# Attention into routed experts into SwiGLU: attention's loads on two queues, and the first expert slot started within attention's last steps

## The chip, the cores and the metric

One core of a Trainium2 chip runs the whole kernel as one program. The metric is the device time of one execution in microseconds (us); lower is better. The engines are named as in the profile: PE (TensorE matmul), PEld (its weight load), DVE (VectorE), ACT (ScalarE), POOL (GpSimd, which also issues DMAs), SP (SyncE, which here only issues DMAs and reads registers).

## The reference

Three layers follow one another. Shapes: 4 batches, 8 heads, 576 positions, head size 64, so 2304 tokens of width 512.

```python
# 1. attention: heads 0-3 see the last 32 positions, heads 4-7 every 32nd position
scores = q @ k.T / 8, masked (local or strided), softmax over keys
x = attn @ v                                  # -> [2304, 512]
# 2. one expert of 8 for each token
e_idx = argmax(x @ w_gate + modality_bias[modality_id])
gate_w = softmax(...)[e_idx]
out[mask_e] = gate_w * (relu(x[mask_e] @ w1[e]) @ w2[e])     # w1 512x1024, w2 1024x512
# 3. SwiGLU on the RMS-normalised rows
xn = x / rms(x) * rms_g
out = (silu(xn @ w_gate2) * (xn @ w_val)) @ w_out            # 512 -> 1536 -> 512
```

## The kernel before

**Attention** runs over 32 steps. There are 8 units, a batch with its local heads (even units) or its strided heads (odd units); a unit has two head pairs, a pair two halves, and each (unit, pair, half) is a step. The loop at the end of `attention` has j from 0 to 34: with i = j - 2 it issues `p_transpose(i)`, `scores(j)`, `qk_transpose(j+2)`, a call of `task(j, 0)`, `av(i)`, `x_transpose(i-1)`, `softmax(j)` and `task(j, 1)`. Every engine works its instructions in the order in which the program issues them, so this loop is the order of the engines. "Step n" below is the stretch that begins with the mask matmul (L148) of `scores(n)`.

**Loads.** `load_qk(n)` and `load_v(n)` load q and k, or v, of pair n (0 to 15). All of them are issued by SP, in one queue. A q or k load is one DMA of 144 KB per head. A local v takes two DMAs per head, a strided v five per head (L96: four of 31.5 KB, one of 18 KB), ten for a pair. `load_v` is called with three pairs ahead (three `vt` buffers), pairs 0, 1 and 2 ahead of the first step. Four small loads for the router (`setup`: `g_sb`, `wg_sb`, `idi`, `b01`) are issued in step 0. POOL issues the stores of attention's output, `xd<-xr` (L212, L216).

**Side work.** When a batch is complete (`on_batch`), a generator starts that routes its tokens (`route`) and, from the second batch on, fills the table of an expert slot (`table_a`). `Side.step` advances the generators at each `task`; a number behind `yield` is the ticks to wait, two ticks a step. While attention runs their small operations go to POOL; in the steps behind the last scores (`over` set) they go to DVE. `table_a(0)` ends with `fetch_known`, which issues slot 0's first weight loads (`raw`, 1 MB each, two buffers, L838) on SP, then computes the slot's token list and gathers its x (`xg`, L843, POOL).

**Slot 0.** A slot is 512 tokens of one expert. `first_slot` splits weight chunks into high and low parts (`conv`, ACT `whi` L908 and DVE `wlo` L909), transposes the gathered x with PE (L899) and splits it (`x_part`: ACT `xhi`, DVE `xlo`). Then the slot loop computes 8 column chunks (`h_chunk`, L1000, 12 matmuls each) and 8 row chunks (`y_chunk`), with `conv` running six chunks ahead. In the steps behind the last scores, PE gets a dummy matmul (`busy`, L247) per step. Four more slots and a loop of variable length follow, then the SwiGLU stage.

## Time and profile before

| What | us |
|---|---|
| Median of 3 runs (847.76 to 850.15) | 848.25 |
| The profiled execution's own time | 851.77 |
| Its span | 850.1 |
| PE busy in the span | 820.1 (96%) |
| DVE, ACT, POOL busy | 498.9, 344.8, 168.6 |
| Step 0 to the first slot's first matmul | 7.83 to 150.26 |

The profile is one execution. Times within it count from the start of the span. A PE that is shown busy can still run at a lower clock: the granted clock stands beside it, 1.00 for 2.4 GHz and 0.50 for 1.2 GHz. A wait is read from who ended it, and the stretch in which it lies says what it is worth.

### The profile page before, as it was taken

What the parts mean: (1) busy time and instruction counts of PE and PEld (TensorE: products, weight loads), DVE (VectorE), ACT (ScalarE), POOL (GpSimd) and SP (SyncE); (2) the same over time, 40 slices, a digit from 0 to 9 for tenths busy, and PEclk for the clock granted to TensorE, in tenths of its full rate; (3) what the DMA queues carried; (4) which work ended last, traced back from release to release, by engine and by line L of the source; (5) the groups of instructions that cost most, each with busy time, mean ns of one, the idle gap of its engine ahead of it and who ended that gap; (6) DMA issues with size and microseconds to landing.
All of it is one profiled execution on the core that took longest, in us unless ns stands there. A gap on an engine that the chain in (4) does not pass through costs nothing.

```text
span 850.1 us, 12584 instructions
## 1 busy us (share of the span) xinstructions
PE 820.1 (96%) x4697; PEld 572.9 (67%) x4697; DVE 498.9 (59%) x1017; ACT 344.8 (41%) x748; POOL 168.6 (20%) x306
## 2 busy tenths in 40 slices
PE   9899997999997999999999999999999999999996
PEld 6788886787885888877566555655655565455565
DVE  4477767675434668575344465755756575564443
ACT  5477774435343564676252323231322323221111
POOL 4135565100202142021000100111111010112201
PEclk9699997999998999999999999999999999999999
DMA  8889575432518465263300101111111011001101
GB/s 141 150 167 176 126 176 152 149 100 101 199 49 283 137 228 198 100 211 87 101 26 1 50 2 48 50 51 49 51 50 36 15 53 47 1 1 74 62 26 62
DMA packets 94806, 80.48 MB, mean 95 GB/s; under 512 B 67990, under 2 KB 68502, under 8 KB 94742
## 3 DMA queue, kind: packets, MB, share of 16 engines
q1 hardware_dynamic: 87990, 64.89, 27.5%
q0 software_dynamic: 6752, 14.75, 5.6%
q8 instruction: 39, 0.64, 0.3%
q14 instruction: 25, 0.20, 0.1%
HBM read 64.84 MB, written 14.75 MB: 94 GB/s over the span
## 4 chain that ended last, share of the span: by engine, by line
PE 56%; issue 6%; DVE 2%; ACT 2%; DMA 2%; POOL 1%; SPq 0%; POOLq 0%; ACTq 0%
PE pg L1258 14%; PE ph L1258 13%; PE po L1292 5%; PE po L1290 5%; PE po L1291 5%; PE ph L1000 5%; PE py L1015 3%; PE py L1017 3%; PE py L1016 3%; DMA yd<-yb 1%; POOL out_dram L1301 1%; PE px L1115 1%; DVE u L1273 1%; ACT dt L435 1%; PE px L899 0%
## 5 line engine op out<-in xcount | busy, mean ns | idle before, releaser
L1277 ACT ACTIVATE ah<-u 128x512 fp32r<-128x512 f32 (+1 forms) x60 | 35.2, 587 | 273.2 <-DVE u L1273 273.2
L377 POOL TENSOR_TENSOR dt<-dt,ds 128x1024 int32<-128x1024 int32 x18 | 43.8, 2434 | 291.9 <-DVE dt L373 291.9
L1290 PE MATMUL po<-woh,ah 128*128 128x512 f32 x216 | 95.0, 440 | 0.2 <-ACT ah L1277 0.2
L1296 DVE TENSOR_TENSOR acc<-po,acc 128x512 f32<-128x512 f32 x72 | 49.6, 690 | 72.7 <-PE po L1292 72.7
L1292 PE MATMUL po<-woh,al 128*128 128x512 f32 x216 | 85.9, 398 | 0.0
L1291 PE MATMUL po<-wol,ah 128*128 128x512 f32 x216 | 85.2, 394 | 0.0
L1258 PEld LDWEIGHTS <-w1h 128*128 128x128 f16 x480 | 46.9, 99 | 46.3 <-ACT w1h L454 1.6
L1258 PEld LDWEIGHTS <-w0h 128*128 128x128 f16 x480 | 42.5, 99 | 49.4 <-issue 15.5
L1000 PE MATMUL ph<-xhi,whi 128*128 128x512 f32 x160 | 65.0, 406 | 6.2 <-SPq L869 5.7
L909 DVE TENSOR_TENSOR wlo<-raw,whi 128x512 fp32r<-128x512 f32 x80 | 60.8, 763 | 15.4 <-ACT whi L908 15.2
L1015 PE MATMUL py<-whi,hh 128*128 128x512 f32 x160 | 65.3, 408 | 0.0
L1000 PE MATMUL ph<-xlo,whi 128*128 128x512 f32 x160 | 63.9, 399 | 0.6 <-DVE xlo L902 0.6
L1000 PE MATMUL ph<-xhi,wlo 128*128 128x512 f32 x160 | 63.6, 398 | 0.0
L1017 PE MATMUL py<-whi,hl 128*128 128x512 f32 x160 | 62.9, 393 | 0.0
L1016 PE MATMUL py<-wlo,hh 128*128 128x512 f32 x160 | 62.6, 391 | 0.0
L1278 DVE TENSOR_TENSOR al<-u,ah 128x512 fp32r<-128x512 f32 (+1 forms) x60 | 38.3, 639 | 40.7 <-ACT ah L1277 40.7
L908 ACT ACTIVATE whi<-raw 128x512 fp32r<-128x512 f32 x80 | 49.5, 626 | 20.1 <-PE py L1017 16.3
L1007 DVE SCALAR_TENSOR_TENSOR hl<-ph,hh 128x512 fp32r<-128x512 f32 x40 | 27.6, 689 | 47.6 <-ACT hh L1006 47.4
L1290 PEld LDWEIGHTS po<-woh,ah 128*128 128x128 f32 x216 | 40.8, 189 | 12.9 <-ACT ah L1277 0.6
L169 ACT ACTIVATE P<-ps,nm 96x128 f32<-96x128 f32 (+1 forms) x176 | 48.4, 375 | 0.0
L1292 PEld LDWEIGHTS po<-woh,al 128*128 128x128 f32 x216 | 40.6, 188 | 10.8 <-DVE al L1278 1.5
L1006 ACT ACTIVATE hh<-ph 128x512 fp32r<-128x512 f32 x40 | 23.9, 598 | 56.6 <-PE ph L1000 54.9
(484 smaller groups left out, 1843.3 us busy)
## 6 DMA issues: line engine op xcount, KB each, us to landing
raw<-in_moe_w_dram SPq DMA_DIRECT2D x20, 1024.0 KB
w<-in_moe_w_gate_dram SPq DMA_DIRECT2D x6, 1024.0 KB
w<-in_moe_w_val_dram SPq DMA_DIRECT2D x6, 1024.0 KB
w<-in_moe_w_out_dram SPq DMA_DIRECT2D x6, 1024.0 KB
yd<-yb SPq DMA_DIRECT2D x5, 1030.0 KB
xg<-yd SPq DMA_DIRECT2D x18, 257.5 KB
qt<-in_q_dram SPq DMA_DIRECT2D x32, 144.0 KB
kt<-in_k_dram SPq DMA_DIRECT2D x32, 144.0 KB
```

The source lines that it names most:

```text
L169: nc.scalar.activation(P[0:nq, hh, t, 0:nk], pv[:, hh, t, :], AF.Exp, bias=nm[0:nq, hh, t:t + 1])
L908: nc.scalar.activation(hi, src, AF.Copy)
L909: eng.tensor_tensor(out=lo, in0=src, in1=hi.bitcast(F32), op=ALU.subtract)
L1000: nc.tensor.matmul(ps, a[:, kk, :], b_[:, kk, :], start=n == 0, stop=n == 3 * KD - 1)
L1015: nc.tensor.matmul(ys[t], hh[:, sl_], whi, start=m == 0, stop=False)
L1016: nc.tensor.matmul(ys[t], hh[:, sl_], wlo, start=False, stop=False)
L1017: nc.tensor.matmul(ys[t], hl[:, sl_], whi, start=False, stop=m == KF - 1)
L1258: nc.tensor.matmul(ps[:, 0:w], a[:, kk, 128 * mc:128 * mc + 128], b_[:, kk], start=i == 0, stop=i == 3 * KD - 1)
L1290: nc.tensor.matmul(ps, ah[:, sl_], woh, start=mc == 0, stop=False)
L1291: nc.tensor.matmul(ps, ah[:, sl_], wol, start=False, stop=False)
L1292: nc.tensor.matmul(ps, al[:, sl_], woh, start=False, stop=mc == MC - 1)
L1296: V.tensor_tensor(out=acc[:, t], in0=ps, in1=acc[:, t], op=ALU.add)
```

## The change

- Strided v loads are split: for the second head of a pair, in batches 0 to 2, POOL issues the five DMAs; SP keeps the rest.
- v is loaded four pairs ahead (four `vt` buffers). Pairs 2 and 3 are not loaded ahead of the first step but behind `load_qk(3)` and `load_qk(4)`, in steps 0 and 1. The four router loads move from step 0 to step 2, their first use from step 6 to step 7.
- The weight fetch of slot 0 becomes a generator of its own, `weights`, that waits until the last v load has been issued (`on_loaded`).
- Three `yield` counts in `route` and `table_a` are one tick shorter, and `first_slot` starts 6 ticks behind the gather instead of 8.
- `first_slot` now does the x transposes first. In the steps behind the last scores `task` runs `filler`: the first two column chunks (`FILL` = 2) of slot 0 in four pieces of six matmuls, between `p_transpose`, `av` and `x_transpose`, with attention's own PSUM banks. The slot loop takes these two chunks as done. The three dummy matmuls there are gone. `over` is set only when attention has ended, so `table_a(1)` runs on POOL.

```diff
@@ load_v
-            vt = v_t[u, hp] = ld.tile([128, 2, 6, D + 1], F32, name="vt", bufs=3)
+            vt = v_t[u, hp] = ld.tile([128, 2, 6, D + 1], F32, name="vt", bufs=4)
...
-                        nc.sync.dma_start(vt[0:18 * (R0[g + 1] - R0[g]), hh, g, 0:D],
-                                          v[b, h0 + hh].rearrange("(m r) d -> r m d", r=32)[R0[g]:R0[g + 1]])
+                        eng = nc.gpsimd if hh and b < B - 1 else nc.sync
+                        eng.dma_start(vt[0:18 * (R0[g + 1] - R0[g]), hh, g, 0:D],
+                                      v[b, h0 + hh].rearrange("(m r) d -> r m d", r=32)[R0[g]:R0[g + 1]])
@@ attention's loop
     load_v(1)
-    load_v(2)
...
                     load_qk(2 * steps[jj][0] + steps[jj][1] + 3)
-        task(j, 0, j >= NS)
+                    if jj in (1, 3):
+                        load_v(jj // 2 + 2)
+        if j < NS:
+            task(j, 0, False)
+        elif i < NS:
+            task(j, 0, True)
         if 0 <= i < NS:
             av(i)
             if steps[i][2] == 1:
-                load_v(2 * steps[i][0] + steps[i][1] + 3)
+                load_v(2 * steps[i][0] + steps[i][1] + 4)
+                if 2 * steps[i][0] + steps[i][1] + 5 == 2 * len(units):
+                    on_loaded()
+        if j >= NS and i < NS:
+            task(j, 1, True)
...
-        task(j, 1, j >= NS)
-        if j < 4 or j >= NS:
+        if j < NS:
+            task(j, 1, False)
+        if j < 4:
             busy(1)
@@ route: yield 4 -> 3; table_a: yield 3 -> 2, yield 4 -> 3
+        def weights(s):
+
+            while not loaded:
+                yield
+            known[0] = s + 1
+            fetch_known()
@@ table_a
-            known[0] = s + 1
-            fetch_known()
+            side.add(weights(s))
...
-                side.add(first_slot(), 8)
+                side.add(first_slot(), 6)
 
         def first_slot():
-            for i in range(AHEAD - 2):
-                conv(i)
-                yield 2
             xt[0] = x_new(xg.pop(0))
             for kk in range(KD):
                 x_part(xt[0], kk, bank)
-                yield 2
-            for i in range(AHEAD - 2, AHEAD):
+                if kk >= KD - FILL:
+                    conv(kk - KD + FILL)
+                yield
+            first_done.append(1)
+            for i in range(FILL, AHEAD):
                 conv(i)
                 yield
             first_done.append(1)
+
+        FILL = 2
+        NS_ = 4 * q.shape[0] * 2
+
+        def filler():
+            for m in range(FILL):
+                ps = bank()
+                xhi, xlo = xt[0][:2]
+                whi, wlo = conv_t.pop(m)
+                n = 0
+                for kk in range(KD):
+                    for a, b_ in ((whi, xhi), (whi, xlo), (wlo, xhi)):
+                        nc.tensor.matmul(ps, a[:, kk, :], b_[:, kk, :], start=n == 0, stop=n == 3 * KD - 1)
+                        n += 1
+                    if kk < KD - 1:
+                        yield
...
@@ task
-                if last and not over:
-                    over.append(1)
+                if last:
+                    if not fill:
+                        while not first_done:
+                            side.step(9)
+                        fill.append(filler())
+                    for _ in range((2, 2, 2, 2, 0)[2 * (j - NS_) + place]):
+                        next(fill[0], None)
+                    side.step(3)
+                    return
...
-                if j == 0:
+                if j == 2:
                     early.append(setup())
-                if j == 6:
+                if j == 7:
                     setup2(*early.pop())
@@ the slot loop
-                h.append(h_chunk(m, xt[s], conv_t.pop(i), tick))
+                if s == 0 and m < FILL:
+                    h.append(filled[m])
+                else:
+                    h.append(h_chunk(m, xt[s], conv_t.pop(i), tick))
```

The first place is SP's queue at the start, behind the loads of pairs 0 to 2 of q and k and of pairs 0 and 1 of v (`vt` is v, `qt` and `kt` are q and k; a number marks the buffer). Before, from the second head of v's pair 2 on:

```order
L96 DMA vt_240<-in_v_dram 126x1x64 x4
L96 DMA vt_240<-in_v_dram 72x1x64
L83 DMA qt_296<-in_q_dram 96x6x64 x2
L83 DMA kt_299<-in_k_dram 96x6x64 x2
L544 DMA g_sb_66<-in_moe2_rms_g_dram 128x4x1
L545 DMA wg_sb_114<-in_moe_w_gate_dram 128x4x8
L547 DMA idi_316<-in_moe_modality_id_dram 128x18x1
L549 DMA b01_318<-in_moe_modality_bias_dram 128x16
```

The same place of the changed kernel, directly behind v's pair 1:

```order
L83 DMA qt_284<-in_q_dram 96x6x64 x2
L83 DMA kt_287<-in_k_dram 96x6x64 x2
L97 DMA vt_290<-in_v_dram 126x1x64 x4
L97 DMA vt_290<-in_v_dram 72x1x64
L83 DMA qt_344<-in_q_dram 96x6x64 x2
L83 DMA kt_347<-in_k_dram 96x6x64 x2
L97 DMA vt_350<-in_v_dram 126x1x64 x4
L97 DMA vt_350<-in_v_dram 72x1x64
L554 DMA g_sb_66<-in_moe2_rms_g_dram 128x4x1
L555 DMA wg_sb_114<-in_moe_w_gate_dram 128x4x8
L557 DMA idi_407<-in_moe_modality_id_dram 128x18x1
L559 DMA b01_409<-in_moe_modality_bias_dram 128x16
```

q and k of pair 3 now stand ahead of all strided v, each strided pair has five DMAs here instead of ten, and the router loads stand behind q and k of pair 4.

The second place is PE behind the last scores (`P` and `PT` are the softmax output and its transpose, `xr` attention's output, `po` its PSUM bank). Before:

```order
L195 MATMUL po<-vt,PT 126x65 x2
L195 MATMUL po<-vt,PT 72x65 x2
L228 MATMUL pt<-ident,xr 128x126 x3
L181 MATMUL pt<-ident,P 126x126 x6
L195 MATMUL po<-vt,PT 126x65 x6
L228 MATMUL pt<-ident,xr 128x126
L228 MATMUL pt<-ident,xr 128x72
L247 LDWEIGHTS ones_b
L247 MATMUL pt<-ones_b 128x512
```

The same place of the changed kernel (`xg` is the gathered x of slot 0, numbered by token tile):

```order
L937 MATMUL pt<-ident,xg_2222 128x128
L196 MATMUL po<-vt,PT 126x65 x2
L196 MATMUL po<-vt,PT 72x65 x2
L229 MATMUL pt<-ident,xr 128x126 x3
L182 MATMUL pt<-ident,P 126x126 x6
L803 MATMUL pt<-xhi,whi 128x512
L803 MATMUL pt<-xlo,whi 128x512
L803 MATMUL pt<-xhi,wlo 128x512
```

The transposes of x, which stood behind all of attention, stand in steps 29 to 31, and chunk matmuls (L803, 24 in all, six at a time) between the last `p_transpose`, `av` and `x_transpose`.

The third place is DVE in steps 31 and 32. Before:

```order
L182 COPY PT<-pt 126x2x126 x2
L160 TENSOR_REDUCE nm<-ps 126x2x2
L203 TENSOR_SCALAR rs<-po 126x2
L204 RECIPROCAL rs<-rs 126x2
L205 TENSOR_TENSOR xr<-po,rs 126x128
L203 TENSOR_SCALAR rs<-po 72x2
L204 RECIPROCAL rs<-rs 72x2
L205 TENSOR_TENSOR xr<-po,rs 72x128
L182 COPY PT<-pt 126x3x126 x2
L909 TENSOR_TENSOR wlo<-raw,whi 128x512
```

The same place of the changed kernel, from `PT` of step 29 to shortly before that of step 30:

```order
L183 COPY PT<-pt 126x2x126 x2
L161 TENSOR_REDUCE nm<-ps 126x2x2
L681 RECIPROCAL wt<-sg 128x5
L684 TENSOR_SCALAR ao<-i128h,ra 128x128 x5
L940 TENSOR_TENSOR xlo<-pt,xhi 128x512
L947 TENSOR_TENSOR wlo<-raw,whi 128x512
L204 TENSOR_SCALAR rs<-po 126x2
L205 RECIPROCAL rs<-rs 126x2
L206 TENSOR_TENSOR xr<-po,rs 126x128
```

The splits of x and of the weights, and the last batch's `wt` and `ao`, now lie between attention's own operations.

## Rows read from the trace of the kernel before

**Rows 1.** PE's waits, 0 to 300 us: total, times, longest

```profile
PE ph L1000 <- SPq L869: 5.7, 1, 5.7
PE po L195 <- DMA vt<-in_v_dram: 3.8, 2, 2.3
PE pt L113 <- DMA kt<-in_k_dram: 2.1, 1, 2.1
PE pt L113 <- DMA qt<-in_q_dram: 1.9, 1, 1.9
```

**Rows 2.** Stretches: length, busy us (instructions) by engine, PEclk, DMA share, GB/s

```profile
20.69:43.89 23.20, 19.24 (x152) 17.07 (x151) 11.15 (x32) 11.21 (x34) 4.19 (x8) 0.71 0.86 149
20.69:30.53 9.84, 5.88 (x44) 5.18 (x43) 2.98 (x8) 3.52 (x11) 0.85 (x2) 0.65 0.98 154
30.53:36.67 6.14, 6.14 (x40) 5.59 (x39) 2.65 (x7) 3.50 (x11) 0.91 (x2) 0.50 0.79 133
59.19:73.67 14.48, 14.21 (x160) 12.66 (x159) 11.17 (x35) 11.35 (x38) 8.08 (x23) 1.00 0.61 131
47.60:77.38 29.78, 29.51 (x350) 25.82 (x349) 22.58 (x67) 22.95 (x75) 13.35 (x33) 1.00 0.74 153
128.27:157.63 29.36, 23.80 (x146) 18.44 (x144) 22.85 (x86) 13.44 (x33) 12.04 (x30) 0.83 0.45 137
139.20:147.28 8.08, 7.43 (x32) 5.48 (x33) 5.44 (x23) 2.33 (x5) 5.31 (x10) 0.53 0.21 44
201.62:204.42 2.80, 2.80 (x13) 2.26 (x12) 0.69 (x2) 1.35 (x3) 0.00 (x0) 1.00 0.00 0
```

**Rows 3.** SP's issues in order of time: start, length, line, operation, tiles

```profile
12.25 8.04 SPq L96 DMA_DIRECT2D vt<-in_v_dram  x10
20.42 0.93 SPq L83 DMA_DIRECT2D qt<-in_q_dram  x2
21.44 1.01 SPq L83 DMA_DIRECT2D kt<-in_k_dram  x2
...
124.46 1.02 SPq L838 DMA_DIRECT2D raw<-in_moe_w_dram  x2
125.59 13.55 SPq L96 DMA_DIRECT2D vt<-in_v_dram  x10
```

**Rows 4.** Two stretches of the start, columns as in rows 2

```profile
16.00:18.00 2.00, 2.00 (x26) 1.63 (x24) 1.54 (x5) 1.86 (x7) 0.33 (x1) 1.00 0.12 27
24.00:26.00 2.00, 0.64 (x3) 0.34 (x3) 0.00 (x0) 0.71 (x1) 0.00 (x0) 0.50 1.10 95
```

**Rows 5.** PE in order of time: slot 0's first and third column chunk

```profile
150.26 0.47 PE L1000 MATMUL ph<-xhi,whi 128*128 128x512 f32 x1
...
157.63 0.50 PE L1000 MATMUL ph<-xhi,whi 128*128 128x512 f32 x1 [0.52 <-DVE hl L1007]
```

**Rows 6.** DVE by line, 128.2 to 158.4 us: busy us, mean ns, idle before

```profile
L909 DVE TENSOR_TENSOR wlo<-raw,whi 128x512 fp32r<-128x512 f32 x8 | 5.5, 693 | 0.3 <-ACT whi L908 0.3
L182 DVE COPY PT<-pt 126x378 f32<-126x378 f32 (+1 forms) x8 | 3.6, 478 | 0.2 <-PE pt L181 0.2
L205 DVE TENSOR_TENSOR xr<-po,rs 126x384 f32<-126x384 f32 (+2 forms) x6 | 2.3, 379 | 0.2
L160 DVE TENSOR_REDUCE nm<-ps 126x6 f32<-126x756 f32 (+1 forms) x2 | 1.6, 809 | 0.1
L204 DVE RECIPROCAL rs<-rs 126x6 f32<-126x6 f32 (+2 forms) x6 | 1.0, 173 | 0.2
L203 DVE TENSOR_SCALAR rs<-po 126x6 f32<-126x6 f32 (+2 forms) x6 | 0.9, 157 | 4.3 <-PE po L195 4.2
```

**Rows 7.** POOL's DMA issues by line: ns min/median/max; the gather's time to landing

```profile
L212 POOL DMA_DIRECT2D xd<-xr x40: 605/622/709, 41.8 to 147.0; - x40
...
L843 POOL DMA_INDIRECT xg<-xd,idxA x8: 946/974/1201, 120.3 to 164.2; - x8
...
DMA to landing us min/median/max: 3.6/4.5/7.6
```

More of the change, by code (lines that the diff above doesn't have):

```diff
@@ L54, in make_consts, with attention @@
     return c
-def attention(ctx, tc, c, wk, q, k, v, xd, xcols, on_batch, task, set_banks):
+def attention(ctx, tc, c, wk, q, k, v, xd, xcols, on_batch, on_loaded, task, set_banks):
     nc = tc.nc
@@ L669, in route @@
             G.tensor_tensor(out=ra[:, t0:t1], in0=ra[:, t0:t1], in1=r1, op=ALU.add)
-            yield 4
+            yield 3
             V.reciprocal(wt[:, t0:t1, 0], sg)
@@ L724, in table_a @@
             G.tensor_tensor(out=base, in0=inc, in1=av, op=ALU.subtract)
-            yield 3
+            yield 2
             V.tensor_scalar(out=base, in0=base, scalar1=1.0, scalar2=None, op0=ALU.min)
@@ L738, in table_a @@
             G.tensor_tensor(out=early_n, in0=early_n, in1=new, op=ALU.add)
-            yield 4
+            yield 3
             blk = small("blka", NA)[:, 0:nt]
@@ L773, in first_slot @@
             first_done.append(1)
+        FILL = 2
[12 more added lines that the diff above has]
+                        yield
+                hh, hl = [xp.tile([128, XW], F32, name="xn", bufs=4)[:, 0:TS].bitcast(F32R) for p in "hl"]
+                nc.scalar.activation(hh, ps, AF.Relu)
+                V.scalar_tensor_tensor(out=hl, in0=ps, scalar=0.0, in1=hh.bitcast(F32), op0=ALU.max, op1=ALU.subtract)
+                filled.append((hh, hl))
+                yield
         def table_b(bank):
@@ L848 @@
         regs, raw_t, conv_t, xg, xt = {}, {}, {}, {}, {}
-        late, first_done, a_done = [], [], []
+        late, first_done, a_done, filled, fill, loaded = [], [], [], [], [], []
         known, waiting = [0], [0, 1]
@@ L966, in task @@
                     return
-                if j == 0:
+                if j == 2:
                     early.append(setup())
-                if j == 6:
+                if j == 7:
                     setup2(*early.pop())
                 side.step(3)
-            attention(pa, tc, c, wk, q, k, v, xd, xcols, on_batch, task, set_banks)
-            while not first_done:
+            attention(pa, tc, c, wk, q, k, v, xd, xcols, on_batch, lambda: loaded.append(1), task, set_banks)
+            over.append(1)
+            assert len(filled) == FILL
+            while len(first_done) < 2:
                 side.step(9)
```

## The prediction

> **What bounds the kernel now.** I read PE's waits first [rows 1], then the stretches around them [rows 2], then the queue that each wait names [rows 3, 4], and last the engines that share the end of attention [rows 5 to 7]. PE is the bound, with 820 of 850 us busy, and in the first 300 us it waits in three places only. At the start it waits 1.9 and 2.1 us for q and k of pair 3; near attention's end 3.8 us for v; and 5.7 us where the loop of variable length is entered, which the change doesn't touch [rows 1]. The reader is to see that the first two waits cost far more than their length. Steps 4 to 7 take 23.20 us; steps 12 to 15, the same work a batch later, take 14.48 [rows 2]. The difference is 8.7 us: 4.0 of it are the waits, the rest is the clock, which is 0.65 over the stretch with the wait and 0.50 over the 6.14 us behind it. At attention's end it is the same picture: behind the waits for v the clock is 0.53 for 8 us [rows 2].
>
> Both waits come from SP's queue. At 12.25 us SP begins ten DMAs of one strided v pair and needs 8.04 us to issue them, 0.80 each; q and k of pair 3 stand behind them and are issued at 20.42 and 21.44 [rows 3]. Meanwhile the DMA engines have little to do: from 16 to 18 us their share is 0.12 [rows 4]. So the shortage there is issue time, not bandwidth. At the end the order is the other way round: the last pair's v is issued behind 2 MB of weights and takes 13.55 us [rows 3].
>
> **The start.** q and k of pair 3 now directly follow v of pair 1, at about 12.25 us instead of 20.42: 8.2 us earlier, against waits of 4.0 us. With five DMAs instead of ten, v's pair 2 takes SP 4.0 us, so q and k of pair 4 stand at about 18.3. POOL issues the other half. The router's loads, in whose time the engines are full (share 1.10) at only 95 GB/s [rows 4], move behind q and k of pair 4 and no longer compete with pair 3. If both waits go, the clock has no reason to fall and the stretch returns to 14.48: 8.7 us. I take 8.0, since more loads now compete in the first 25 us. Bounds: 2 us, if half of the waits stays and the clock falls as before, and 9 us.
>
> **The second queue.** POOL gets 30 issues more, 5 for each of six pairs. The nearest row is its store of `xr`, of the same shape: 0.62 us, 0.71 at most [rows 7]. In a batch that is 6.2 us on top of 13.35 of 29.78 [rows 2], so POOL stays below two thirds; at the dearest row, the gather's 1.20 us, it would be 25.4, still below 29.78. These loads wait only for buffers that PE has just released, and are needed eight steps (29.8 us) later. I count nothing; POOL's own slack hides it. The Trainium skill speaks against it: "SBUF — State Buffer", section "SBUF: two separate sides", says that GpSimd can't write a DMA's descriptors while VectorE runs certain copies, and gives about 620 ns alone and 3100 ns beside one. The trace disagrees here: 40 issues lie between 605 and 709 ns while DVE is busy 22.58 of 29.78 us. By the page the 30 issues would be 93 us, an estimate, instead of 19; what that would do is the last rival.
>
> **The middle of attention.** Three `yield` counts are a tick shorter, so DVE asks POOL half a step (1.86 us) earlier for the ranks and tables, and what stands behind on DVE, the copy of `PT` for PE's next `av`, waits with it. DVE has 7.2 us idle in a batch. I take a loss of 0.5 us; bounds are nothing and 5.6 us (three times 1.86). A gain is excluded, since PE's work is the same.
>
> **Weights behind v.** The last two v pairs are issued in steps 23 and 25: 20 DMAs at 0.80 us, 16.1 us, or 4.3 steps of 3.72 us. The weights follow in step 27 to 28, earlier than before. Their first `wlo` stands in step 30, two to three steps later (some 9 us). All waits for v at the end go; next late would be these weights, or the gather. The gather is issued some 1.5 steps earlier than before, and the first x transposes ask for it three steps later, 11 us, where it takes 4.5 us to land, 7.6 at most [rows 7], behind 4 issues of about 1 us. Covered by some 2 us at worst.
>
> **The tail.** Measure from the scores of step 30 to the third column chunk: before, 128.27 to 157.63, 29.36 us [rows 2, 5]. In the changed kernel the same span holds the same PE work, now interleaved. Two floors:
> - PE: 23.80 us busy, of which 7.43 at a clock of 0.53; at full clock about 20.3.
> - DVE, by its new order: eleven 512-wide splits at 0.69 (7.6), eight `PT` copies at 0.478 (3.8), two maxima at 0.81 (1.6), six groups of sum, reciprocal and product at 0.709 (4.3), eight small ones at 0.16 (1.3): 18.6 us [rows 6].
>
> DVE can't run through: each filled chunk's split waits for its last six matmuls (1.4 us each, from 2.80 for twelve [rows 2]), and the last `x_transpose` waits for the last `xr`, about 1 us. That makes 22.4. PE also waits for DVE inside, at `av` of step 30, whose `PT` stands behind two weight splits and one x split: some 2 us, too short and too late to add to the DVE sum. One x transpose and the last batch's counting matmuls move ahead of my starting point, 1.0 us. The gain is 29.36 - 22.4 - 1.0 = 6.0 us. Bounds: 9.8, with DVE's bare 18.6, and nothing, if the waits bring the clock to half again.
>
> Behind that, the slot loop does two chunks less, so the generator that prepares the later slots has some six ticks less cover. It ends at the same place in the order as before, and its weights are converted six chunks (16.8 us) ahead of use. I count nothing; without that cover it would be two chunks, 5.6 us. The other edits (three dummy matmuls gone, `table_a(1)` on POOL) are in the sums.
>
> **Sum.** 8.0 - 0.5 + 6.0 = 13.5 us. The profiled execution would go from 851.77 to 838.3; the median shown is 3.5 us lower, and the same gain there gives 848.25 - 13.5 = 834.75, rounded 834.8.
>
> **Rivals.**
> - The tail gives nothing: DVE becomes the bound of steps 30 to 33, PE waits in pieces for `PT` and `xlo`, and the clock falls as it did at 139 us. For it: 18.6 us of DVE beside 20.3 of PE, both in one chain. Against it: no single wait should reach the 3.8 us of before. Only the start is left: 848.25 - 8.0 + 0.5 = 840.8.
> - The start stays bound by transfer: two queues bring no more bytes, and the late q and k are only replaced by late v. It gains 2, and the sum is 2 - 0.5 + 6.0 = 7.5: 840.8 too. Against it: the share of 0.12 [rows 4]. The Trainium skill, "DMA: Bandwidth & Descriptors", section "Issuing engines are not separate DMA queues", says that issuing from several engines saves only issue time, since all run on the same 16 DMA engines. By that rule a start short of bandwidth would give this time; the trace says issue time is what is short, so it decides nothing against the forecast.
> - The waits only move: v or x late in new places of the same weight. No change, about 848.
> - Slower: POOL's queue falls behind. POOL has 16.4 us idle in a batch; ten more issues fit while each takes less than 1.64 us. Above that POOL falls behind in each of two batches; ranks and stores come late, DVE stands waiting for POOL, and PE behind it. It turns the result at 2.3 us each, where two times 6.8 us make up the gain; at 2.6 us it is 9.6 us a batch, 19 in all, 834.8 + 19 = 854. Against it: 0.71 at most [rows 7].
>
> **How the numbers follow.** The forecast, with its own range of 830 to 839, gets 0.62. The tail without gain gets 0.16, the start without 0.10, waits that only move 0.05, POOL's queue 0.07. The first three are faster by more than 0.3% (2.5 us, about what a measurement of this kernel can tell from no change): 0.88. Within it: 0.05. Slower: 0.07. The range for 8 in 10 reaches from 829.5, the better bounds of both ends nearly together, to 842, which takes in the two rivals with half the gain.
>
> **What would show it.** Right: no wait for `qt` or `kt` near 22 us and a clock of 1.00 from 10 to 40 us; steps 4 to 7 near 14.5 us; no wait of `po` for `vt`; third column chunk some 13 us earlier than 157.6; POOL's v issues near 0.62 us. Wrong: a clock of 0.5 anywhere ahead of the third chunk, a wait of PE for DVE above 3 us in steps 30 to 33, `whi` or the x transposes waiting for DMA, or a longer wait behind the first slots that gives the gain back.

## The result, and the profile after

| | median | lowest to highest | profiled execution | its span |
|---|---|---|---|---|
| before | 848.02 us | 847.76 to 850.15 | 851.77 us | 850.1 us |
| after | 836.12 us | 835.58 to 838.78 | 838.78 us | 836.9 us |

With a fourth run the median before is 848.02 us, where the prediction had 848.25 of three.

The ratio is 0.986 (95% interval 0.9834 to 0.9887): 11.9 us faster, against 13.5 us forecast. The profiled execution lies 3.7 us above its median before and 2.7 after, so the traces differ by a little more, 13.2 us of span. The experiments further down ran on four chips on which the kernel before takes 857 to 859 us (below, the chip of this first measurement is called the first chip; at 848 us it is hardly one of the four). There the mean granted clock of one and the same kernel changes from execution to execution (before: 0.967 to 0.988), so single times spread by some 10 us, and only ratios to the kernel before, taken on the same chip, are compared (0.1% is 0.86 us).

**The waits.** PE's waits of the first 300 us in the kernel after (engine, tile and line, what it waited for; us in total, times, longest), to be held against [rows 1]:

```profile
PE ph L1047 <- SPq L907: 6.0, 1, 6.0
PE pt L937 <- DVE xlo L940: 1.8, 2, 1.3
PE pt L182 <- ACT xTb L236: 1.8, 2, 1.2
...
PE po L196 <- POOL ia L694: 1.1, 1, 1.1
PE pt L114 <- DVE PT L183: 0.7, 1, 0.7
...
PE pt L114 <- DMA qt<-in_q_dram: 0.2, 1, 0.2
```

The waits for `kt` and `vt` are gone, the one for `qt` is 0.2 us. The wait at the entry of the loop of variable length stays (6.0, before 5.7). New are the short ones for VectorE and ScalarE in attention's last steps, none above 1.3 us.

**The stretches.** The kernel after by stretches: from the scores of step 4 to those of step 8, on to step 26, to step 30, to the third column chunk, and the rest (columns: stretch, length, busy us and instructions of PE, PEld, DVE, ACT and POOL, PE's clock, DMA share, GB/s):

```profile
22.33:36.05 13.72, 13.72 (x153) 12.36 (x151) 10.19 (x28) 10.94 (x34) 4.15 (x8) 1.00 0.69 127
36.05:103.19 67.14, 66.34 (x779) 58.12 (x778) 52.31 (x165) 50.78 (x163) 46.07 (x112) 1.00 0.95 186
103.19:121.83 18.64, 17.87 (x217) 15.15 (x216) 12.06 (x37) 13.82 (x43) 7.74 (x11) 1.00 0.62 174
121.83:144.57 22.74, 17.72 (x130) 14.12 (x128) 16.50 (x47) 10.66 (x28) 16.84 (x49) 1.00 0.38 121
144.57:836.87 692.30, 675.59 (x3272) 452.93 (x3270) 395.29 (x705) 246.60 (x453) 101.40 (x129) 0.99 0.24 81
```

The first row answers to the 23.20 us and the fourth to the 29.36 us of [rows 2]. PE's clock is 1.00 in every stretch up to the third chunk, where before it was 0.65, 0.50 and 0.53 in places. PE has 5.0 us free in the fourth stretch, in pieces of at most 1.35 us, and the clock stays at 1.00 beside them.

**The queues.** SP's issues in the kernel after, at the start and at attention's end (start, duration, queue and line, tile, count), and below them all DMAs of the strided v by queue (min/median/max ns):

```profile
12.44 1.50 SPq L83 DMA_DIRECT2D qt<-in_q_dram  x2
14.04 1.73 SPq L83 DMA_DIRECT2D kt<-in_k_dram  x2
15.81 4.11 SPq L97 DMA_DIRECT2D vt<-in_v_dram  x5
20.04 1.83 SPq L83 DMA_DIRECT2D qt<-in_q_dram  x2
...
98.26 16.19 SPq L97 DMA_DIRECT2D vt<-in_v_dram  x20
116.90 31.69 SPq L876 DMA_DIRECT2D raw<-in_moe_w_dram  x4
```

```profile
L97 SPq DMA_DIRECT2D vt<-in_v_dram x50: 655/748/1003, 15.8 to 113.8; - x50
L97 POOL DMA_DIRECT2D vt<-in_v_dram x30: 597/626/852, 9.9 to 78.0; - x30
```

q and k of pair 3 go 8 us earlier than in [rows 3]. The last v pairs go ahead of the weights. An issue on POOL costs what its row of before let expect (0.62 us, [rows 7]).

**Where the time went**, worked out from the starts of the scores of each step in the two traces:

| stretch | before | after | gain |
|---|---|---|---|
| start to step 0 | 7.83 | 9.24 | -1.4 |
| step 0 to 4 | 12.86 | 13.09 | -0.2 |
| step 4 to 8 | 23.20 | 13.72 | 9.5 |
| step 8 to 26 | 66.54 | 67.14 | -0.6 |
| step 26 to 30 | 17.84 | 18.64 | -0.8 |
| step 30 to third chunk | 29.36 | 22.74 | 6.6 |
| third chunk to end | 692.43 | 692.30 | 0.1 |

The 1.4 us ahead of step 0 is not the change's: the last six dummy matmuls of the warm-up took 2.77 us in this execution and 1.53 before. In all experiments below step 0 begins between 7.4 and 7.8 us, also in those that start exactly as the changed kernel does.

### The profile page after: what moved, and what is told of

Same layout as the page of the kernel before. It is cut to its first block, busy times and chain, and to the rows that moved or that the text cites. A ratio compares the mean times of both kernels' runs of the same rounds, so it can differ in the third digit from the quotient of the medians.

```text
span 836.9 us, 12580 instructions
## 1 busy us (share of the span) xinstructions
PE 812.0 (97%) x4694; PEld 566.0 (68%) x4694; DVE 494.5 (59%) x997; ACT 344.4 (41%) x748; POOL 191.8 (23%) x356
## 4 chain that ended last, share of the span: by engine, by line
PE 59%; issue 6%; DVE 2%; POOL 1%; ACT 1%; DMA 1%; SPq 0%; POOLq 0%; ACTq 0%
PE pg L1308 14%; PE ph L1308 13%; PE ph L1047 7%; PE po L1342 5%; PE po L1340 5%; PE po L1341 5%; PE py L1062 3%; PE py L1064 3%; PE py L1063 3%; POOL out_dram L1351 1%; DMA yd<-yb 1%; PE px L1162 1%; DVE u L1323 1%; ACT dt L445 1%; PE px L937 0%
## 5 line engine op out<-in xcount | busy, mean ns | idle before, releaser
L1047 PE MATMUL ph<-xhi,whi 128*128 128x512 f32 x152 | 62.3, 410 | 6.0 <-SPq L907 6.0
L1062 PE MATMUL py<-whi,hh 128*128 128x512 f32 x152 | 62.0, 408 | 0.0
L1047 PE MATMUL ph<-xlo,whi 128*128 128x512 f32 x152 | 61.0, 401 | 0.0
L1047 PE MATMUL ph<-xhi,wlo 128*128 128x512 f32 x152 | 60.9, 401 | 0.0
L1064 PE MATMUL py<-whi,hl 128*128 128x512 f32 x152 | 59.7, 393 | 0.0
L1063 PE MATMUL py<-wlo,hh 128*128 128x512 f32 x152 | 59.5, 392 | 0.0
L1341 PEld LDWEIGHTS po<-wol,ah 128*128 128x128 f32 x216 | 40.7, 188 | 8.2
```

Of the source, the lines that this page charges most:

```text
L1047: nc.tensor.matmul(ps, a[:, kk, :], b_[:, kk, :], start=n == 0, stop=n == 3 * KD - 1)
L1062: nc.tensor.matmul(ys[t], hh[:, sl_], whi, start=m == 0, stop=False)
L1063: nc.tensor.matmul(ys[t], hh[:, sl_], wlo, start=False, stop=False)
L1064: nc.tensor.matmul(ys[t], hl[:, sl_], whi, start=False, stop=m == KF - 1)
L1341: nc.tensor.matmul(ps, ah[:, sl_], wol, start=False, stop=False)
```

## The experiments

Ratios are to the kernel before on the same chip, with their 95% intervals; times forecast in the expectations stand for a chip on which the kernel before takes 848 us. e1 to e4 ran on one chip, e5 to e8 on a second, e9 to e11 on a third, e12 on a fourth.

| run | ratio | interval | step 4 to 8 | step 8 to 26 | step 26 to third chunk, clock there |
|---|---|---|---|---|---|
| before (first chip) | 1 | | 23.20 | 66.54 | 47.20, 0.89 |
| after (first chip) | 0.986 | 0.983 to 0.989 | 13.72 | 67.14 | 41.38, 1.00 |
| e1 second queue alone | 0.992 | 0.989 to 0.996 | 13.82 | 69.47 | 48.62, 0.89 |
| e2 order alone, one queue | 0.999 | 0.996 to 1.003 | 13.96 | 81.83 | 50.29, 0.82 |
| e3 all of the loads | 0.990 | 0.983 to 0.996 | 13.73 | 67.33 | 45.30, 0.96 |
| e4 the end alone | 0.997 | 0.994 to 1.000 | 22.44 | 67.14 | 49.70, 0.83 |
| e5 the changed kernel again | 0.984 | 0.979 to 0.989 | 13.72 | 67.09 | 45.68, 0.93 |
| e6 without the two chunks | 0.989 | 0.984 to 0.993 | 13.72 | 67.23 | other work, see there |
| e7 all v on POOL | 0.994 | 0.990 to 0.998 | 14.07 | 72.13 | 43.45, 1.00 |
| e8 old yields | 0.985 | 0.978 to 0.991 | 13.72 | 66.68 | 46.56, 0.89 |
| e9 gather two and two, no gap | 0.982 | 0.978 to 0.985 | 13.81 | 67.23 | 44.87, 0.96 |
| e10 plain loads for the gather | 0.977 | 0.974 to 0.980 | 13.72 | 66.96 | 42.55, 0.92 |
| e11 router's loads early | 0.985 | 0.981 to 0.989 | 15.37 | 66.86 | 48.21, 0.86 |
| e12 gather two and two, with a gap | 0.975 | 0.973 to 0.978 | 13.72 | 67.06 | 43.60, 0.96 |

**e1: the second queue alone.** The kernel before with

```
-                        nc.sync.dma_start(vt[...], v[...])
+                        eng = nc.gpsimd if hh and b < B - 1 else nc.sync
+                        eng.dma_start(vt[...], v[...])
```

> The kernel before with one edit: five of the ten DMAs of each strided v pair (all but the last batch) are issued by POOL. Order of all loads, number of buffers and the end of attention as before. Theory (issue time on SP is what the first batch lacks): v of pair 2 takes SP 4.0 us in place of 8.04, so q and k of pair 3 are issued 4 us earlier, about 16.4 and 17.4 in place of 20.4 and 21.4; the two waits of 1.9 and 2.1 us shrink to a trace, the clock stays at 1.00, and most of the start's 8 to 9 us is gained by this edit alone: 839 to 841. Rival (order decides): the extra bytes in flight ahead of pair 3 and the router's loads behind it keep q and k late; at least one wait of over 1 us stays, and the gain is 0 to 3 us: 845 to 848.

SP's issues in e1 at the start, and its two stretches from step 4 to 8 and from step 8 to 26:

```profile
12.16 4.13 SPq L97 DMA_DIRECT2D vt<-in_v_dram  x5
16.42 0.93 SPq L83 DMA_DIRECT2D qt<-in_q_dram  x2
17.45 1.00 SPq L83 DMA_DIRECT2D kt<-in_k_dram  x2
```

```profile
20.44:34.26 13.82, 13.82 (x154) 12.45 (x152) 10.72 (x32) 10.98 (x34) 7.29 (x13) 1.00 1.05 165
34.26:103.73 69.47, 67.00 (x772) 57.87 (x770) 51.12 (x151) 50.66 (x163) 44.64 (x109) 1.00 0.86 173
```

The theory holds: with nothing but the issue time halved, q and k leave 4 us earlier, PE has no wait for them, and the start is as short as in the changed kernel, although the order and the router's loads are as before and the DMA share there is 1.05. What is lost behind, 2.9 us in the middle, sits in two steps (13 and 21) where ScalarE waits 1.85 and 1.83 us for POOL's `ex`; in e3, with the loads in the new order, it is gone. So the other edits of the loads (the order, the fourth buffer, the router's loads) have their worth too, but in the middle and not at the start; which of them it is was not run apart.

**e2: the new order with one queue.** The changed kernel with

```
-                        eng = nc.gpsimd if hh and b < B - 1 else nc.sync
+                        eng = nc.sync
```

> The changed kernel with the second queue taken away: all ten DMAs of every v pair on SP, in the new order, four pairs ahead. Theory (the order is worth most, the second queue little): q and k of pair 3 are issued at 12.4 us as in the changed kernel, so no wait for them; v of pair 2 now takes 8 us of SP, q and k of pair 4 stand at 24 in place of 20, v of pair 3 ends at 35 us and is first needed near 36: one short wait of 1 to 2 us there, 2 to 4 us over the changed kernel's time, 838 to 840. Rival (the second queue is what pays): the wait only moves to pair 4's q and k or pair 3's v, with the clock at half behind it as before, 6 to 9 us over the changed kernel, 842 to 845.

SP's issues in e2, and the stretches from step 4 to 8 and from step 8 to 9:

```profile
14.98 8.00 SPq L97 DMA_DIRECT2D vt<-in_v_dram  x10
23.09 0.94 SPq L83 DMA_DIRECT2D qt<-in_q_dram  x2
24.13 1.00 SPq L83 DMA_DIRECT2D kt<-in_k_dram  x2
25.17 7.81 SPq L97 DMA_DIRECT2D vt<-in_v_dram  x10
...
36.56 0.93 SPq L83 DMA_DIRECT2D qt<-in_q_dram  x2
```

```profile
20.49:34.45 13.96, 13.92 (x153) 12.40 (x152) 9.01 (x22) 10.97 (x34) 4.18 (x8) 1.00 0.50 117
34.45:46.34 11.89, 6.21 (x40) 5.46 (x39) 4.87 (x18) 2.70 (x10) 1.36 (x3) 0.69 1.08 159
```

The rival holds, and more than it says: of the gain nothing is left that can be measured. q and k of pair 3 are in time, but q and k of pair 5 stand behind twice 8 us of v and the router's loads; PE waits 4.8 us for them, the clock falls, and step 8 takes 11.89 us in place of 3.7 (before). The wait has moved by four steps with all that it costs. From step 24 to 30 the steps take about 7 us again; there PE waits 1.7 us for k and 2.2 us for ScalarE's `xTb`. The order alone only chooses which load is late; the second queue is what takes the lateness away.

**e3: all edits of the loads, nothing of the end.** The kernel before with e1's edit and

```
-vt = ... ld.tile([128, 2, 6, D + 1], F32, name="vt", bufs=3)
+vt = ... ld.tile([128, 2, 6, D + 1], F32, name="vt", bufs=4)
-    load_v(2)
+                    if jj in (1, 3):
+                        load_v(jj // 2 + 2)
-                load_v(2 * steps[i][0] + steps[i][1] + 3)
+                load_v(2 * steps[i][0] + steps[i][1] + 4)
-                if j == 0: ...setup()      if j == 6: setup2(...)
+                if j == 2: ...setup()      if j == 7: setup2(...)
```

> The kernel before with all edits of the loads (five of ten v DMAs on POOL, the new order at the start, four v buffers and four pairs ahead, the router's loads two steps later), and nothing of the end: no column chunks within attention, yields and dummy matmuls as before. Theory (the two parts add up): the start gains about 9 us, as the traces of before and after compare, and the wait of 3.8 us for v at attention's end goes too, but PE then waits for VectorE in steps 30 to 33; the third column chunk comes 10 to 11 us earlier than before, 837.5 to 839.5. Rival (the end's whole gain came from v, not from the chunks moved into it): the time is that of the changed kernel, 836. Second rival (the wait for v only hid VectorE's): the end gains nothing, 839.5 to 841.

0.990, which is the theory's 839 us on its scale; the rivals' 0.986 and 0.991 lie within the interval as well, so the time alone does not tell them apart. The trace helps: steps 4 to 8 take 13.73 us, and from step 30 to the third chunk it is 24.69 us, 1.95 more than in the changed kernel and 4.67 less than before. So by these profiles the loads alone bring the larger part of what is gained behind step 30 too, since v of the last pairs is there in time. From step 26 on the picture is another: e3 takes 45.30 us and the changed kernel, run again in e5, 45.68. What e5 has shorter behind step 30 it has longer ahead of it, where steps 26 to 30 take 20.61 us in e3 and 22.93 in e5. Some of this is work that moved ahead of step 30 (0.8 us on the first chip); the rest lies where both have the stop at the gather that e9 to e12 are about.

**e4: the end without the loads.** The changed kernel with e2's edit, and order, buffers and router's loads at the start set back (the edits of e3 the other way round).

> The changed kernel with the loads of the start as before: v three pairs ahead, all on SP, v of pair 2 ahead of q and k of pair 3, the router's loads at step 0. Kept: the weights wait for the last v, x and two column chunks within attention's last steps, the shorter yields, the dummy matmuls left out. Theory (two separate gains): the waits for q and k of pair 3 are back with their clock, so the start's 9 us are lost, and the end's gain of about 6 us stays: 842 to 844. Rival (the end needs v four pairs ahead): with v of the last pair issued two steps later, the wait for it or for the weights behind it comes back, and the gain is under 3 us: 845 to 848.

The theory's first half holds: the waits for q and k are back (2.9 and 1.4 us) and steps 4 to 8 take 22.44 us. The time, 0.997, is the rival's 845 to 848 on its scale, but the rival's cause is not in the trace: PE waits neither for `vt` nor for the weights, though the last 20 DMAs of v take SP until 129 us and the weights leave at 131. From step 30 to the third chunk it takes 22.26 us, as little as the changed kernel. What is lost lies ahead of step 30: steps 26 to 30 take 27.44 us (17.84 before, on the first chip), and this begins beside the first slot's gather. VectorE stands still for 4.36 us, until 1.2 us behind the end of the last issue; PE is busy 1.70 of the 4 us from 118 on, and then the clock is low until 136 us:

```profile
121.36 0.16 DVE L204 TENSOR_SCALAR rs<-po 96x6 f32<-96x6 f32 x1 [4.36 <-remote]
```

```profile
118.00:122.00 4.00, 1.70 (x17) 1.30 (x16) 0.58 (x3) 1.01 (x5) 1.82 (x2) 0.89 0.82 218
118.00:136.00 18.00, 15.38 (x106) 13.18 (x105) 7.28 (x24) 7.28 (x23) 3.65 (x6) 0.59 0.55 136
137.42:159.68 22.26, 17.73 (x129) 14.11 (x128) 16.69 (x47) 9.68 (x25) 15.86 (x47) 0.98 0.35 110
```

So e4 does not show that the end needs the new loads. Loads alone and end alone give 0.990 and 0.997, together (e5) 0.984. The intervals are wide, so whether the step from 0.987 (their product) to 0.984 is real, and the two parts help each other, stays open.

**e5: the changed kernel again**, without an edit.

> The changed kernel itself, unedited, once more beside the kernel before, as the measure for the other runs of this group and for the parts run apart so far (queue alone 0.992 of before's time, loads alone 0.990, end alone 0.997, all in one queue 0.999). Theory (the parts support each other): 0.986 of before again, the clock at 1.00 from 10 us to the third column chunk. Rival (the end is on the edge of the clock): at least one stretch at half clock between 100 and 145 us, and 0.990 or more.

0.984: the result holds on another chip, where the kernel before takes 9 us more. The clock however is not at 1.00 throughout, as the rival had it: 0.93 between step 26 and the third chunk, with half clock from 114 to 116 us. What stands ahead of it is told at e9 to e12.

**e6: the chunks taken out.** The changed kernel with

```
-        FILL = 2
+        FILL = 0
```

> The changed kernel with the two column chunks taken out of attention's last steps (they follow behind attention as before); x of the first slot stays within these steps, as do the loads. Theory (the chunks fill gaps in which PE waits for VectorE): PE's gaps in steps 30 to 33 stay empty, the 5.6 us of two chunks follow behind, the third chunk comes 3 to 6 us later and the time is 3 to 6 us longer than the changed kernel's; a fall of the clock there may come on top. Rival (VectorE bounds these steps, and PE's work there is hidden anyway or does not fit): within 1 us of the changed kernel.

Its median is 848.35 us beside the changed kernel's 843.21 on the same chip: 5.1 us slower, 3.9 by the ratios (their intervals overlap), within the theory's 3 to 6. From step 29 (119.88) to its first chunk behind attention:

```profile
119.88:146.47 26.59, 21.04 (x156) 17.66 (x155) 17.66 (x55) 13.59 (x36) 16.22 (x49) 0.76 0.16 38
```

PE has 5.5 us of gaps and a clock of 0.76 here, and the two chunks still to do. The gaps that the chunks fill are real. e6 has neither the chunks nor the dummy matmuls that stood there before, so part of its loss can be the clock; the two were not told apart.

**e7: all strided v on POOL.** The changed kernel with

```
-                        eng = nc.gpsimd if hh and b < B - 1 else nc.sync
+                        eng = nc.gpsimd if b < B - 1 else nc.sync
```

> The changed kernel with all ten DMAs of each strided v pair (all but the last batch) on POOL, so POOL issues 60 in place of 30. Theory (POOL has slack, an issue takes it 0.6 to 0.7 us whatever VectorE does): 6.5 us more per batch fit into its 16.4 us of idle time less the 6.2 already taken; within 1.5 us of the changed kernel. Rival (POOL's queue falls behind): the stores of xr and the rank counting wait behind ten issues in a row (6.5 us, almost two steps), PE or VectorE waits for POOL, and the time is 3 us or more longer, beginning in the first batches. By the rule of the Trainium skill's page SBUF — State Buffer, section SBUF: two separate sides, an issue would take up to 3.1 us in the time in which VectorE copies; the time would then be far above that of the kernel before.

The rival's time holds: 0.994, some 8 us more than the changed kernel. The two profiled executions differ by 6.1 us, 5.0 of them in the middle (72.13 in place of 67.09 us from step 8 to 26), and there in one step, step 13 (8.41 in place of 3.30). The issues by queue, and the waits between 50 and 66 us:

```profile
L97 POOL DMA_DIRECT2D vt<-in_v_dram x60: 597/632/852, 9.9 to 84.9; - x60
```

```profile
DVE rs L204 <- PE po L196: 6.0, 3, 5.2
ACT ex L665 <- POOL ex L651: 4.5, 1, 4.5
...
PE pt L114 <- ACT xTb L240: 3.5, 1, 3.5
```

An issue is as short as before. But the ten in a row stand in POOL's program ahead of `ex` and last from 47.57 to 55.76 us, ScalarE waits 4.5 us for `ex` with all of its own later work behind it, and PE waits 3.5 us for that. POOL stands still between its issues, 1.9 us in this row and 5.7 us in all in the first 100 us, until earlier DMAs of its own have landed:

```profile
POOL vt L97 <- DMA vt<-in_v_dram: 4.3, 7, 1.5
...
POOL vt L97 <- DMA xd<-xr: 1.4, 3, 0.7
```

In the changed kernel no v issue waits so (its list has two stores of `xr` that wait for a landing v, 2.9 us together; before has one, 4.0 us). A batch later the same row stands ahead of the same operation, goes out without such waits, and ScalarE does not wait for `ex`:

```profile
79.56 6.07 POOL L97 DMA_DIRECT2D vt<-in_v_dram  x10
```

```profile
87.34 0.23 ACT L665 ACTIVATE ex<-ex 128x32 f32<-128x32 f32 x1
```

So the sum over a batch, which POOL would have had the time for, does not decide, and neither does the number of issues in the row alone: step 13 became 5 us longer where the ten took 8.2 us, and where they took 6.1 nothing waited.

**e8: the old yields.** The changed kernel with the counts 3, 2 and 3 set back to 4, 3 and 4.

> The changed kernel with the three shortened yields set back (4, 3 and 4 ticks), all else kept. Theory (middle loss of about 0.5 us from asking POOL half a step too early): 0.5 us faster to 1 us slower than the changed kernel, that is, not to be told from it. Rival (the shorter yields are what brings the gather in time): the ranks and tables come up to one and a half ticks later, the x transposes of the first slot start later or wait for their gather, and the third chunk comes 2 to 5 us later.

0.985 against 0.984: not to be told apart, as the theory says. From step 8 to 26 it is 0.4 us shorter (66.68 in place of 67.09), from there to the third chunk 0.9 us longer (46.56 in place of 45.68); the gather goes out 4 us later (the first at 110.68 in place of 106.60). Most of the difference in the middle is work that has moved and no wait: with the old yields PE does seven instructions fewer there (772 against 779) and is busy 0.29 us less (66.13 against 66.42).

**e9 and e10: the gather.** In e5, and in every run on these chips that has the gather, VectorE, ScalarE or both stand still while POOL issues it. e9 sends it two and two:

```
-            slot_x(s)
+            if s == 0:
+                xg[0] = [x_fetch(idxA, t, 128 * CUT[2], t) for t in (0, 1)]
+                yield
+                xg[0] += [x_fetch(idxA, t, 128 * CUT[2], t) for t in (2, 3)]
+                side.add(first_slot(), 5)
```

> The changed kernel with the first slot's four gathers issued two and two, one tick (half a step) apart, in place of four in a row; the first x transposes stay at the same place of the order. In six of the eight experiments so far VectorE and ScalarE both stand still from some point within the four gathers until about 1 us behind the end of the last one's issue (up to 5.2 and 4.4 us), and PE's clock falls right behind. Theory (the run of indirect issues on POOL holds both engines up): with two and two, each stop is 1 to 2.5 us long, PE waits less, fewer stretches at half clock between 100 and 135 us; 0 to 4 us faster than the changed kernel, ratio 0.980 to 0.985. Rival (the stops have another cause, and the later gather costs): one stop stays, of the same length, or the x transposes wait for the gather; the same time or up to 2 us slower.

e10 has four plain loads there:

```
+                    nc.gpsimd.dma_start(g[:, 0:XW], xd[128 * t:128 * t + 128])
```

> The changed kernel with the first slot's gather left out: x of that slot is loaded as the first 512 rows in a row by four plain POOL DMAs at the same place in place of four indirect ones (a part of the computation changed: the first slot works on the wrong tokens). Theory (the indirect issues hold VectorE and ScalarE up): no stop of both engines over 2 us between 100 and 130 us, and no half clock there; 3 to 6 us faster than the changed kernel on a chip that shows the stops, within 1 us on one that does not. Rival (something else there does it, weights or v in flight): the stops stay where they are.

POOL, ScalarE and VectorE around the gather in e5 (last gather; first instruction behind the stop of each; in brackets how long the engine had been idle, and what ended that; "remote" where the profile names no instruction):

```profile
110.52 0.95 POOL L881 DMA_INDIRECT xg<-xd,idxA  x1 [0.30 <-issue]
...
112.99 0.26 ACT L627 COPY lt<-pt 32x128 f32<-32x128 f32 x1 [3.90 <-remote]
...
113.11 0.16 DVE L204 TENSOR_SCALAR rs<-po 96x6 f32<-96x6 f32 x1 [4.78 <-remote]
```

The same places in e10:

```profile
105.91 2.21 POOL L778 DMA_DIRECT2D xg<-xd  x4
...
109.98 0.40 ACT L240 COPY xTb<-pt 128x288 f32<-128x288 f32 x1 [1.16 <-PE pt L229]
...
109.72 0.16 DVE L204 TENSOR_SCALAR rs<-po 96x6 f32<-96x6 f32 x1 [1.76 <-PE po L196]
```

And in the kernel after on the first chip:

```profile
112.38 0.95 POOL L881 DMA_INDIRECT xg<-xd,idxA  x1 [0.30 <-issue]
...
112.23 0.40 ACT L240 COPY xTb<-pt 128x288 f32<-128x288 f32 x1 [1.16 <-PE pt L229]
...
111.97 0.16 DVE L204 TENSOR_SCALAR rs<-po 96x6 f32<-96x6 f32 x1 [1.77 <-issue]
```

e10's theory holds, in one profiled execution: without the indirect issues the engines' idle times are the ordinary ones, 1.16 and 1.76 us, and the ratio is 0.977 in place of 0.984 (beside e9, on e10's own chip and with the gather, 0.982; their intervals overlap). Its clock between step 26 and the third chunk still averages 0.92, since one fall comes later (behind 126 us); only the one at the gather is gone. The first chip had the same four gathers and no stop at all. e9 did not test what it was meant to: no other POOL instruction stood between the pairs, so the four went out in a row (106.81 to 111.67), the stop was as long as in e5 (ScalarE 5.1, VectorE 5.8 us), and its 0.982 is not to be told from 0.984.

**e11: the router's loads early.** The changed kernel with `setup` at step 0 and `setup2` at step 6, as before.

> The changed kernel with the router's loads set back two steps (ahead of q and k of pair 4 on SP), all else kept. Theory (issue time on SP is what the start lacks, and with half of v on POOL there is enough of it): q and k of pair 4 go about 3 us later, at 24 in place of 20.4, and are needed near 28.6; a wait under 1.5 us or none, and 0 to 2 us more than the changed kernel. Rival (the router's small elements clog the DMA engines): they hold up q and k of pair 4 and v of pair 2 by more than their issue time; a wait of over 2 us and the clock at half behind it, 4 us or more.

PE's only waits for DMA from 10 to 50 us:

```profile
PE pt L114 <- DMA kt<-in_k_dram: 1.1, 1, 1.1
PE pt L114 <- DMA qt<-in_q_dram: 0.3, 1, 0.3
```

The theory holds: 1.4 us of waits, 1.65 us in steps 4 to 8, no half clock in these steps, and 0.985, the changed kernel's ratio within the intervals. With half of v on POOL, moving the router's loads is worth little.

**e12: the gather with a real gap.** e9's edit with `yield 2`, which puts a store of `xr`, and with it a wait for VectorE, between the two pairs.

> The changed kernel with the first slot's four gathers two and two, now with a store of xr between the pairs in POOL's order (a store that waits for VectorE), so that POOL really leaves a gap; with one tick between them, as run before, no other POOL instruction stood between and the four went out in a row. The first x transposes come up to half a step later. The run with plain loads in their place gave 0.977 of before's time, the changed kernel 0.984 beside the same chip. Theory (VectorE and ScalarE stay stopped until about 1 us behind the last indirect issue of a row): the first stop ends near 110 us, where VectorE would wait for PE anyway, the second is 1 to 3 us long; less of the clock is lost and the ratio is 0.978 to 0.983. Rival (each row of issues makes a stop of its own, whatever its length, or the later x costs as much): two stops of 2 us and more, 0.983 to 0.988.

0.975, the lowest of all versions that do the whole work, with an interval (0.973 to 0.978) that lies below those of both runs of the changed kernel and does not touch that of e11. It was not run beside the changed kernel on one chip, so its lead over it, 7 to 9 us by the ratios, is not measured directly. The trace does not go as the theory has it:

```profile
107.73 0.16 DVE L204 TENSOR_SCALAR rs<-po 96x6 f32<-96x6 f32 x1 [0.61 <-PE po L196]
...
113.39 0.82 DVE L183 COPY PT<-pt 128x288 f32<-128x288 f32 x2 [4.70 <-remote]
...
113.34 0.27 ACT L627 COPY lt<-pt 128x128 f32<-128x128 f32 x1 [2.93 <-remote]
```

Beside the first pair (106.5 to 108.9) VectorE works on; the one stop is beside the second (110.0 to 112.3) and hardly shorter for VectorE (4.70 in place of 4.78), a microsecond shorter for ScalarE (2.93 in place of 3.90). But it comes one step's work later: `xr`, its store and the softmax of that step are done ahead of it, PE has no single wait above 1.0 us there, and from step 26 to the third chunk it takes 43.60 us in place of 45.68. PE does not run through either: between 109 and 114 us it stands still five times, 2.1 us in all, where the profile names nothing that it waits for, and from 112 to 116 us its clock is 0.70. Why the first pair stops nobody is open.

## Why the prediction was right, step by step

**What bounds the kernel** was read rightly. The waits at 22 us came from SP's issue time, and e1 shows it alone: five of ten issues taken off SP, nothing else changed, and the stretch falls from 23.20 to 13.82 us. That a wait costs more than its length, with the clock low behind it, shows again in e2, where 4.8 and 0.9 us of waits make a step 8.2 us longer.

**The start**: 9.5 us in the stretch, taken as 8.0 with a bound of 9. The size was off because 14.48 us (steps 12 to 15) was used as the floor. It is not the same work: PE has 160 instructions there and 0.3 us of gaps [rows 2], and 153 without a gap in the 13.72 us of after. Between e4, which has the loads of the kernel before at the start (22.44), and e3, which has the new ones (13.73), on one chip, the difference is 8.7. In the profiled execution 1.4 us of this went again ahead of step 0, by chance. Two reasons given for the term carry less than the prediction gives them: the order (e2: the wait moves to pair 5) and the router's loads (e11: 1.65 us, not measurable in the time). The halved issue time carries it.

**The second queue** was counted at nothing as a cost, and that is right: 30 issues at a median of 626 ns, no work waits for them. The Trainium skill, "SBUF — State Buffer", section "SBUF: two separate sides", gives 3100 ns beside VectorE copies of a certain kind; over the 30 issues here and the 60 of e7 the longest is 852 ns, with VectorE busy 52.31 of 67.14 us. The measurement decides for these issues; whether one of VectorE's operations beside them was of that kind no run here shows. "DMA: Bandwidth & Descriptors", section "Issuing engines are not separate DMA queues", says that a second issuing engine saves only issue time; the trace agrees that it is issue time, and here it is not small: without it nothing of the gain is left (e2 0.999, e5 0.984), and by itself it brings half (e1 0.992).

**The middle**: a loss of 0.5 was taken; 0.6 in the trace, and 0.4 by e8 with the yields set back. The size fits, the reason only in part: PE's work in this stretch is not the same, as the prediction has it, but 779 instructions and 66.34 us busy in place of 771 and 66.00, so more than half of the 0.6 is work that moved in.

**Weights behind v**: no wait for `vt`, `raw` or the gather in the trace after, as forecast.

**The tail**: 22.74 us from step 30 to the third chunk, 22.4 forecast, and 0.8 us moved ahead of step 30, 1.0 forecast: 5.8 us gained against 6.0. The wait for `PT` at `av` of step 30, put at some 2 us, is 1.1 (the list names POOL's `ia`, which had long been done). On the first chip the rival that the tail gives nothing is out by this row and its clock of 1.00. The gain is not the chunks' alone: e3, without them, is 4.67 us shorter than before in the same stretch, and e6 puts the chunks at some 4 to 5 us. What the prediction did not see is the stop at the gather. With it steps 26 to 30 take 22.93 us in e5 and 27.44 in e4, against 18.64 on the first chip, and a clock of 0.5 ahead of the third chunk, one of the prediction's signs of being wrong, does come there. The kernel before was not profiled on those chips, so this term is measured on the first chip alone; the whole ratio there (0.984 in e5) is no worse.

**Later slots**: nothing, as counted; 692.43 us before and 692.30 after.

**Sum**: 13.0 us between the two profiled executions (851.77 to 838.78) where 13.5 was forecast. The medians differ by 11.9. The last step of the sum, that the same gain holds between medians, is thus off by 1.1 us: the execution profiled before lay 3.7 us above its median, the one after 2.7. That the 13.0 come so near is in part luck: the start gained 1.5 us more than was taken, and 1.4 went again ahead of step 0.

**The rivals.** A start bound by transfer is out: 13.72 us at a clock of 1.00. That the waits only move is what e2 shows with one queue; with two it did not happen. POOL's queue falling behind did not happen, but its price was worked out wrongly: the prediction let POOL take ten more issues a batch while each takes less than 1.64 us. e7 adds as many again at 0.63 us and loses some 8 us, most of it where ten in a row, drawn out to 8.2 us, stand ahead of `ex`. The point from which it decides is not the sum over a batch but how long a row ahead of something that is waited for really takes.

## What to carry to other kernels

When loads come late while the DMA engines have time, count what each queue needs to issue them: a new order on the same queue only chooses who is late, a second queue takes the lateness away. Compare each row given to the second queue with the slack of what that engine computes next, and count in the pauses within the row; with ten issues in place of five more than half of the gain was given back. Independent work moved into an engine's gaps is worth at most the gaps, and what stops the engines just ahead of them can take as much again.

## What the runs showed of the hardware that was not expected

**A gather's issue can stop other engines.** In the ten experiments that issue the first slot's gathers in a row (on three chips), ScalarE, VectorE or both are idle beside them for longer than in e10, up to 5.8 us, mostly until 0 to 1.6 us behind the end of the last issue (in e1 ScalarE starts 0.4 us ahead of it, in e6 and e11 VectorE 0.5); in e12, on a fourth chip, beside the second pair. With plain loads in the same place it does not happen, and on the first chip not with the gathers either. So by these traces, one execution of each run, the indirect issues are needed for it, and something that differs between chips or executions. The Trainium skill, "SBUF — State Buffer", section "SBUF: two separate sides", lets only GpSimd and VectorE hold each other up and says that ScalarE never waits; here ScalarE stands still too (3.90 us beside VectorE's 4.78 in e5), so a port shared by GpSimd and VectorE does not explain it. Whether it is the signals between engines or their instructions that come late was not settled.

**POOL waits for its own DMAs.** With 60 v issues on it, POOL stood idle ten times, up to 1.5 us, until an earlier DMA from its queue had landed; with 30 no v issue did. Whether the program's semaphores or the queue ask for these waits was not settled.
